# RWKV-6 recurrence and SwiGLU: k's product moves from VectorE to GpSimd, state scaling in one instruction, and a new order

## The chip, the cores and the metric

The kernel runs on one core of one Trainium2 chip. The metric is device time in microseconds: the median of the runs of one kernel. Inside a core five engines run their own instruction streams: PE (TensorE, matrix multiplications), DVE (VectorE), ACT (ScalarE), POOL (GpSimd) and SP (SyncE, which here only issues DMAs). PE writes to PSUM, eight banks of accumulator memory that DVE and ACT read.

## The reference

There are B = 4 batches, H = 8 heads, S = 768 time steps and D = 48 channels per head. For each batch and head a state of 48 x 48 numbers is carried through time, and its output is normalised and passed through a gated feed-forward layer:

```python
cur = np.einsum('bhd,bhe->bhde', u[None] * kt, vt)
y[:, :, t] = np.einsum('bhd,bhde->bhe', rt, state + cur)
state = wt[:, :, :, None] * state + np.einsum('bhd,bhe->bhde', kt, vt)
...
xn = x / np.sqrt(np.mean(x * x, axis=-1, keepdims=True) + 1e-06) * rms_g
g = xn @ w_gate
out = (g / (1.0 + np.exp(-g)) * (xn @ w_val)) @ w_out
```

Here x is y with the heads side by side: 3072 tokens by 384 channels. The hidden width is 1536.

## The kernel before

**Tiling.** Time is cut into six superblocks of 128 steps. A step of work is named `function.n.j`: superblock n (0 to 5), and batch j (0 to 3), or for the feed-forward layer one of 12 slices f of 128 hidden units. One tile holds 128 time steps on the partitions and 8 x 48 = 384 channels.

**The recurrence in matrix form.** The logarithm of w (`ln`) is summed over time by a matmul with a triangular mask (`cs_mm`, lines 350 to 376). This gives the exponent for r in a PSUM bank `ps_a` (line 369), and in four extra columns of the same bank the totals over the whole superblock (four small matmuls, line 372). The exponent for k lies in a bank `ps_b`: superblock 2 gets it by a second matmul with another mask (line 375), superblocks 3 to 5 (`ONE_SUM`) by adding ln w to r's sum on DVE (`cs_add`, line 380). Superblocks 0 and 1 (`WIN`) have their own matmuls. `exp_r` and `exp_k` (ACT, through line 200) take the exponentials: in place in PSUM, but for superblock 1 into SBUF tiles `er` and `ek`. `r_mul` (line 403) and `k_mul` (line 408), both on DVE, multiply r and k by them into the bf16 buffer `rk`. `w_tot` (line 400) copies the four totals into a small tile `wcol`.

**From there.** `rk` is transposed (`rk_tr`: for superblocks 0 and 1 by PE in `rk_pe` and a copy on ACT, later by a DMA on SP's queue, line 436), and `q_mm` (lines 449, 451) forms the products k.r of all pairs of time steps, for even and odd heads. `q_mask_e` (DVE, line 456) masks the even ones; `q_copy_o` (ACT) copies the odd ones out of PSUM and `q_mask_o` (POOL, line 467) masks them. `st_mm` (line 477) forms the sum of k v for the state. `st_new` adds the old state (line 483) and multiplies by the totals, in two DVE instructions of 48 partitions each (line 485): two heads lie together in one matmul, and only the two diagonal blocks are wanted. `y_mm` forms y. POOL computes the u term: `bonus_mul` (r k, then times u: lines 414 and 415), and after DVE's row sum `bonus_sum` (line 419) `bonus_v` (line 424). `x_add` adds both; `x_sq` (ACT), `x_rstd` (POOL, lines 515 and 516; ACT in superblock 0) and `xn_mul` (ACT) normalise. `xn_pe` and `xn_out`, or `xn_tr` and `xn_gain` with a DMA, transpose the result. POOL also casts v to bf16 (`cast_v`, from superblock 2).

**The feed-forward layer.** `gate_mm` and `val_mm` (line 557, three matmuls of 512 columns each) fill banks `ps_a` and `ps_b`; `silu` (ACT) and `h_mul` (DVE, line 575) make the hidden units; `o_mm` (line 620, twelve matmuls for each batch) projects them back, `o_out` copies and `out_dma` stores.

**What sets the order.** The string `ORDER` (lines 25 to 128) lists all 1091 steps. They are issued in just this order, so each engine and each DMA queue works through its own steps of the list, strictly in sequence, and waits where an input is late. The feed-forward layer of superblock n-1 is interleaved with the recurrence of superblock n. The list also has 36 `warm` steps: matmuls on zeros (line 333) which nobody reads. SP's queue carries the loads of r, k, v and w, the DMA transposes and the stores; POOL's queue carries the loads of the weights (`load_gv`, `load_wo`), which stand in POOL's sequence.

**PSUM.** Three pools of banks are handed out in rotation: `psA` (2 banks), `psB` (2) and `psQ` (4), lines 167 to 169.

Of the kernel before, what the change touches and what calls it, by code (L numbers as in the profile page):

```python
# [37 lines left out]
cast_v.0.2 cast_v.0.3 bonus_sum.0.2 bonus_sum.0.3 warm.27.0 x_add.0.0 warm.29.0 x_sq.0.0 load_r.2.3 r_mul.1.0 q_mm.0.2
q_mask_e.0.2 y_mm.0.1 cs_mm.1.1 x_rstd.0.0 exp_k.1.1 xn_mul.0.0 warm.35.0 x_add.0.1 q_mask_o.0.2 warm.34.0 q_mm.0.3
q_mask_e.0.3 x_sq.0.1 exp_r.1.1 x_rstd.0.1 load_k.2.3 y_mm.0.2 bonus_v.0.2 x_add.0.2 x_sq.0.2 xn_mul.0.1 x_rstd.0.2  # L40
xn_mul.0.2 q_mask_o.0.3 cs_mm.1.2 st_mm.0.3 st_mm.0.2 st_new.0.2 xn_pe.0.0 bonus_v.0.3 y_mm.0.3 x_add.0.3 load_gv.1.0
load_gv.1.1 bonus_mul.1.0 xn_out.0.0 xn_pe.0.1 xn_out.0.1 x_sq.0.3 x_rstd.0.3 xn_mul.0.3 xn_pe.0.2 xn_out.0.2 cs_mm.1.3
exp_r.1.3 exp_r.1.2 exp_k.1.3 xn_pe.0.3 st_new.0.3 k_mul.1.0 rk_pe.1.0 rk_tr.1.0 st_mm.0.1 xn_out.0.3 gate_mm.0.0
gate_mm.0.1 exp_k.1.2 q_mm.1.0 val_mm.0.1 k_mul.1.3 r_mul.1.3 silu.0.0 st_new.0.1 val_mm.0.0 rk_pe.1.3 q_mask_e.1.0
h_mul.0.0 k_mul.1.1 q_copy_o.1.0 silu.0.1 h_mul.0.1 gate_mm.0.2 silu.0.2 gate_mm.0.6 silu.0.6 val_mm.0.2 h_mul.0.2
bonus_sum.1.0 gate_mm.0.3 gate_mm.0.5 val_mm.0.3 silu.0.3 h_mul.0.3 cast_v.1.0 st_mm.1.0 gate_mm.0.9 st_new.1.0
silu.0.5 gate_mm.0.4 silu.0.9 r_mul.1.1 val_mm.0.5 h_mul.0.5 bonus_mul.1.3 gate_mm.0.7 rk_tr.1.3 cast_v.1.1 silu.0.4
val_mm.0.4 h_mul.0.4 st_mm.1.1 rk_pe.1.1 st_new.1.1 val_mm.0.9 val_mm.0.6 h_mul.0.6 r_mul.1.2 bonus_v.1.0 q_mask_o.1.0
y_mm.1.0 bonus_mul.1.1 k_mul.1.2 rk_tr.1.1 gate_mm.0.8 silu.0.8 silu.0.7 val_mm.0.7 h_mul.0.7 rk_pe.1.2 rk_tr.1.2
q_mm.1.1 q_copy_o.1.1 gate_mm.0.11 silu.0.11 load_wo.0.0 load_wo.2.0 q_mask_e.1.1 x_add.1.0 bonus_mul.1.2 load_wo.1.0  # L50
val_mm.0.8 h_mul.0.8 h_mul.0.9 q_mm.1.3 q_copy_o.1.3 q_mask_o.1.3 bonus_sum.1.3 q_mm.1.2 q_mask_e.1.2 q_copy_o.1.2
bonus_sum.1.1 gate_mm.0.10 val_mm.0.11 silu.0.10 val_mm.0.10 h_mul.0.10 bonus_sum.1.2 h_mul.0.11 q_mask_o.1.1 y_mm.1.1
x_sq.1.0 q_mask_o.1.2 cast_v.1.2 y_mm.1.2 bonus_v.1.1 x_add.1.1 o_mm.0.0 q_mask_e.1.3 ln.2.0 cs_mm.2.0 ln.2.1 cs_mm.2.1
bonus_v.1.2 x_add.1.2 o_out.0.0 out_dma.0.0 x_rstd.1.0 x_sq.1.1 cast_v.1.3 y_mm.1.3 st_mm.1.3 st_new.1.3 o_mm.0.1
bonus_v.1.3 x_rstd.1.1 x_add.1.3 exp_r.2.0 xn_mul.1.0 xn_pe.1.0 exp_k.2.1 k_mul.2.1 xn_mul.1.1 exp_r.2.1 w_tot.2.1
x_sq.1.2 x_rstd.1.2 r_mul.2.0 xn_out.1.0 w_tot.2.0 st_mm.1.2 st_new.1.2 o_mm.0.2 ln.2.2 cs_mm.2.2 x_sq.1.3 xn_mul.1.2
xn_pe.1.2 exp_k.2.0 k_mul.2.0 rk_tr.2.0 o_out.0.1 xn_pe.1.1 xn_out.1.1 xn_out.1.2 o_mm.0.3 exp_k.2.2 k_mul.2.2
load_v.2.0 r_mul.2.1 rk_tr.2.1 ln.2.3 x_rstd.1.3 exp_r.2.2 w_tot.2.2 xn_mul.1.3 xn_pe.1.3 xn_out.1.3 cs_mm.2.3
exp_r.2.3 r_mul.2.2 r_mul.2.3 w_tot.2.3 exp_k.2.3 k_mul.2.3 load_w.3.0 cast_v.2.1 st_mm.2.1 load_w.3.3 val_mm.1.1
gate_mm.1.1 silu.1.1 h_mul.1.1 o_out.0.2 load_v.2.2 rk_tr.2.3 load_v.4.3 rk_tr.2.2 load_v.2.3 load_k.3.1 load_r.3.1  # L60
o_out.0.3 out_dma.0.3 st_new.2.1 gate_mm.1.0 silu.1.0 val_mm.1.0 h_mul.1.0 bonus_mul.2.1 bonus_sum.2.1 gate_mm.1.5
silu.1.5 gate_mm.1.7 silu.1.7 val_mm.1.5 h_mul.1.5 bonus_mul.2.2 bonus_mul.2.0 bonus_v.2.1 gate_mm.1.3 silu.1.3
q_mm.2.0 q_mask_e.2.0 bonus_sum.2.2 q_mm.2.1 q_mask_e.2.1 gate_mm.1.2 silu.1.2 val_mm.1.2 h_mul.1.2 gate_mm.1.4
cast_v.2.0 st_mm.2.0 st_new.2.0 val_mm.1.3 h_mul.1.3 val_mm.1.4 gate_mm.1.6 bonus_mul.2.3 cast_v.2.2 st_mm.2.2
q_copy_o.2.1 bonus_sum.2.0 silu.1.4 h_mul.1.4 silu.1.6 q_copy_o.2.0 bonus_v.2.2 q_mask_o.2.0 q_mask_o.2.1 bonus_sum.2.3
cast_v.2.3 gate_mm.1.8 st_new.2.2 val_mm.1.7 gate_mm.1.9 h_mul.1.7 val_mm.1.9 y_mm.2.1 x_add.2.1 bonus_v.2.0 silu.1.9
h_mul.1.9 gate_mm.1.10 silu.1.10 y_mm.2.0 x_add.2.0 bonus_mul.3.1 val_mm.1.6 h_mul.1.6 q_mm.2.2 q_copy_o.2.2
q_mask_o.2.2 x_sq.2.0 q_mask_e.2.2 x_rstd.2.0 q_mm.2.3 q_mask_e.2.3 val_mm.1.8 val_mm.1.11 silu.1.8 h_mul.1.8
bonus_sum.3.1 bonus_v.2.3 q_copy_o.2.3 q_mask_o.2.3 load_r.3.0 load_k.3.0 bonus_mul.3.0 gate_mm.1.11 silu.1.11
h_mul.1.11 st_mm.2.3 y_mm.2.2 ln.3.0 val_mm.1.10 h_mul.1.10 o_mm.1.0 x_add.2.2 st_new.2.3 o_out.1.0 xn_mul.2.0 y_mm.2.3  # L70
x_add.2.3 cs_mm.3.0 xn_pe.2.0 cs_add.3.0 load_w.3.1 load_k.3.2 ln.3.1 cs_mm.3.1 cs_add.3.1 xn_out.2.0 out_dma.0.1
load_w.3.2 ln.3.2 x_sq.2.1 x_rstd.2.1 x_sq.2.2 load_k.3.3 out_dma.0.2 load_r.4.1 load_r.3.3 load_v.3.0 out_dma.1.0
load_v.3.2 load_r.3.2 exp_r.3.0 w_tot.3.0 bonus_sum.3.0 r_mul.3.0 ln.3.3 exp_k.3.1 exp_k.3.0 k_mul.3.0 rk_tr.3.0
# [58 lines left out]
def kernel(  # L132
# [42 lines left out]

    def sel(s):
        return {(int(x[0]), int(x[1])) for x in s.split()}

    CAST_ACT = sel("00 01 02 03 10 11 12 13")
    EXPR_SB = sel("10 11 12 13")  # L180
    EXPK_SB = sel("10 11 12 13")
    WIN = (0, 1)
    Q_PAIR = ((4, 2),)
    OLD_DVE = (1, 2, 3, 4)
    ONE_SUM = (3, 4, 5)
    O_IN_A = ()
    XOUT_ACT = sel("")
# [484 lines left out]
```

## Time and profile before

| quantity | value |
|---|---|
| median of 3 runs | 207.44 us (207.34 to 208.61) |
| the profiled execution | 208.67 us, of which the span from first to last instruction is 206.9 us; 1.8 us lie around it |
| mean granted TensorE clock | 0.992 |
| busy | PE 195.5, DVE 159.3, ACT 138.1, POOL 108.9 us |
| k_mul on DVE, 20 from PSUM and 4 from SBUF | 546 and 609 ns each |
| st_new's two multiplies, 40 in all | 354 ns each |
| r k on POOL (line 414), 24 | 999 ns each |
| HBM | 25.96 MB read, 4.72 MB written |

The profile is of one execution. Busy times of PE overlap, since matmuls are pipelined: a matmul's record is longer than the distance to the next one. A line of a group gives line, engine, operation, tiles, shapes and count, then busy us in all, mean ns of one, and the idle time of the engine just before. A line of windows gives the length of a stretch and each engine's busy us in it, with the number of instructions, then the granted clock, the share of the DMA engines and GB/s. A line of the timeline gives start us, length us, engine, line, operation, tiles and count.

The first matmul of line 557 starts at 31.63 us. The first matmul of each superblock's out projection (line 620) starts at 53.78, 84.63, 115.90, 144.73, 172.59 and 195.93 us. The stretches between these marks are called stages here: stage 1 from 53.78 (`o_mm.0.0`), stage 2 from 84.63 (`o_mm.1.0`), stage 3 from 115.90, stage 4 from 144.73, stage 5 from 172.59.

### The profile page before, as it was taken

Reading aid. Unit: us, or ns where it says so; the run is one execution under the profiler, and the core shown is the slowest. Engines: PE = TensorE matmul, PEld = TensorE weight load, DVE = VectorE, ACT = ScalarE, POOL = GpSimd, SP = SyncE. Lnnn points to the kernel's source line nnn. Section 1 sums busy time; section 2 is a strip of 40 time slices with the busy share of each in tenths; the row PEclk is TensorE's granted clock in tenths of the full one; section 3 lists DMA queues with packets and bytes.
Section 4 is the critical chain, followed back from the end, with each engine's and each line's share of the span. In section 5 each row is a group of like instructions: output and inputs, shape, how many; then the busy total and the mean of one; then the engine's idle time right before and its main releaser. Section 6 shows DMA issues by size and latency. Waiting matters only on the chain.

```text
span 206.9 us, 4493 instructions
## 1 busy us (share of the span) xinstructions
PE 195.5 (94%) x1608; PEld 114.8 (55%) x1608; DVE 159.3 (77%) x324; ACT 138.1 (67%) x278; POOL 108.9 (53%) x170
## 2 busy tenths in 40 slices
PE   1999969989999999999999999999999999999994
PEld 1566545555665555665546665556555556555562
DVE  5169895789998899999879999998986676236521
ACT  2587998557997645889557968576976666064400
POOL 6098980390959379739776859738330464000000
PEclk9999997999999999999999999999999999999999
DMA  6999999999996999969989989982128401140013
GB/s 139 287 229 188 186 213 203 189 197 207 202 210 134 204 212 222 204 142 197 204 156 262 196 193 244 199 160 47 22 76 212 105 5 38 38 155 0 0 55 137
DMA packets 121566, 32.41 MB, mean 157 GB/s; under 512 B 116420, under 2 KB 120392, under 8 KB 121544
## 3 DMA queue, kind: packets, MB, share of 16 engines
q1 hardware_dynamic: 119504, 28.58, 64.4%
q0 software_dynamic: 2032, 3.54, 9.4%
q8 instruction: 12, 0.20, 0.4%
q14 instruction: 10, 0.08, 0.1%
q10 hardware_dynamic: 8, 0.00, 0.0%
HBM read 25.96 MB, written 4.72 MB: 148 GB/s over the span
## 4 chain that ended last, share of the span: by engine, by line
PE 50%; DVE 14%; DMA 9%; ACT 9%; POOL 6%; SPq 6%; issue 6%; DVEq 0%; POOLq 0%; ACTq 0%
PE ps_q L620 13%; PE ps_a L557 13%; PE ps_b L557 12%; DMA rt<-in_r_dram 7%; DVE ht L575 3%; SPq L213 3%; DMA vt<-in_v_dram 2%; DVE st L485 2%; PE ps_q L449 2%; ACT xn L520 2%; SPq L226 2%; PE ps_q L431 2%; POOL qts L467 1%; POOL ruk L415 1%; PE ps_q L333 1%
## 5 line engine op out<-in xcount | busy, mean ns | idle before, releaser
L200 ACT ACTIVATE sg<-ps_a 128x512 bf16<-128x512 f32 x72 | 42.1, 598 | 38.3 <-PE ps_a L557 27.9
L575 DVE TENSOR_TENSOR ht<-ps_b,sg 128x512 bf16<-128x512 f32 x72 | 48.6, 686 | 20.6 <-ACT sg L200 10.9
L557 PE MATMUL ps_b<-xnt,wv_sb 128*128 128x512 bf16 x216 | 56.5, 380 | 1.0 <-DVE ht L575 0.7
L557 PE MATMUL ps_a<-xnt,wg_sb 128*128 128x512 bf16 x216 | 56.0, 385 | 0.1
L620 PE MATMUL ps_q<-wo_sb,ht 128*128 128x384 bf16 (+1 forms) x300 | 49.4, 320 | 0.2 <-ACT ob L629 0.2
L620 PEld LDWEIGHTS <-ht 128*128 128x128 bf16 x300 | 28.2, 98 | 17.1 <-issue 0.2
L557 PEld LDWEIGHTS <-wg_sb 128*128 128x128 bf16 x216 | 23.4, 115 | 20.6 <-issue 1.6
L557 PEld LDWEIGHTS <-wv_sb 128*128 128x128 bf16 x216 | 22.9, 114 | 20.2 <-issue 2.6
L414 POOL TENSOR_TENSOR ruk<-rt,kt 128x384 f32<-128x384 f32 x24 | 24.0, 999 | 13.7 <-DVE rk L403 6.3
L424 POOL TENSOR_TENSOR ydiag<-vt,diag 128x384 f32<-128x384 f32 x24 | 20.0, 839 | 12.9 <-DVE diag L419 12.8
L415 POOL TENSOR_TENSOR ruk<-ruk,u_bc 128x384 f32<-128x384 f32 x24 | 24.0, 999 | 1.9
L467 POOL TENSOR_SCALAR_AFFINE_SELECT qts<-qts 128x512 bf16<-128x512 bf16 x20 | 12.4, 634 | 19.0 <-ACT qts L460 19.0
L456 DVE TENSOR_TENSOR qts<-ps_q,mask_lt 128x512 bf16<-128x512 f32 x24 | 16.2, 681 | 1.5 <-PE ps_q L451 1.4
L520 ACT ACTIVATE xn<-xb,rstd 128x384 bf16<-128x384 f32 x24 | 14.4, 611 | 3.8 <-POOL rstd L516 3.6
L502 DVE TENSOR_TENSOR xb<-ps_q,ydiag 128x384 f32<-128x384 f32 x24 | 13.2, 549 | 1.5 <-PE ps_q L497 1.4
L198 ACT ACT_TABLE_LOAD x10 | 12.8, 1283 | 1.8 <-PEq L656 1.6
L419 DVE TENSOR_REDUCE diag<-ruk 128x8 f32<-128x384 f32 x24 | 13.0, 544 | 1.1 <-POOL ruk L415 1.0
L403 DVE TENSOR_TENSOR rk<-rt,ps_a 128x384 bf16<-128x384 f32 x20 | 10.8, 545 | 3.6 <-ACT ps_a L200 3.5
L507 ACT ACTIVATE junk<-xb 128x384 bf16<-128x384 f32 x24 | 12.4, 517 | 1.6 <-DVE xb L502 1.3
L200 ACT ACTIVATE lw<-wt 128x384 bf16<-128x384 f32 (+1 forms) x20 | 11.0, 577 | 3.6 <-DMA wt<-in_w_dram 3.5
L515 POOL TENSOR_SCALAR rstd<-rstd 128x1 f32<-128x1 f32 x20 | 3.8, 190 | 16.5 <-ACT junk L507 15.6
L460 ACT CAST qts<-ps_q 128x512 bf16<-128x512 f32 x20 | 11.3, 585 | 1.0 <-PE ps_q L451 0.8
(83 smaller groups left out, 281.5 us busy)
## 6 DMA issues: line engine op xcount, KB each, us to landing
rt<-in_r_dram SPq DMA_DIRECT2D x24, 192.0 KB, 4.0
kt<-in_k_dram SPq DMA_DIRECT2D x24, 192.0 KB, 3.7
vt<-in_v_dram SPq DMA_DIRECT2D x24, 192.0 KB, 3.6
out_dram<-ob SPq DMA_DIRECT2D x23, 192.0 KB, 2.1
wt<-in_w_dram SPq DMA_DIRECT2D x16, 192.0 KB, 3.6
wt<-in_w_dram SPq DMA_DIRECT2D x4, 384.0 KB, 4.6
wo_sb<-in_moe_w_out_dram POOLq DMA_DIRECT2D x3, 384.0 KB, 7.1
wg_sb<-in_moe_w_gate_dram POOLq DMA_DIRECT2D x1, 768.0 KB, 10.0
```

The costliest lines, as they stand in the source:

```text
L200: return nc.scalar.activation(**kw).ins
L414: nc.gpsimd.tensor_tensor(out=ruk[n, j], in0=inp["r", n, j], in1=inp["k", n, j], op=ALU.mult)
L415: nc.gpsimd.tensor_tensor(out=ruk[n, j], in0=ruk[n, j], in1=u_bc, op=ALU.mult)
L419: nc.vector.tensor_reduce(out=diag[n, j].rearrange("p h o -> p (h o)"), in_=ruk[n, j], axis=mybir.AxisListType.X, op=ALU.add)
L424: nc.gpsimd.tensor_tensor(out=ydiag[n, j], in0=inp["v", n, j], in1=diag[n, j].to_broadcast([128, H, D]), op=ALU.mult)
L456: nc.vector.tensor_tensor(out=qts[n, j][:, 0], in0=bank["q", n, j][0], in1=bc_mid(mask_lt, NP), op=ALU.mult)
L467: nc.gpsimd.affine_select(out=qts[n, j][:, 1], in_=qts[n, j][:, 1], compare_op=ALU.is_gt, fill=0.0, base=0, pattern=[[0, NP], [1, 128]], c ...
L502: nc.vector.tensor_tensor(out=xb[n, j], in0=bank.pop(("y", n, j)), in1=ydiag[n, j].rearrange("p h d -> p (h d)"), op=ALU.add)
L520: nc.scalar.activation(out=xn, in_=xb[n, j], func=AF.Copy, scale=rstd[n, j][:, 1:2])
L557: nc.tensor.matmul(ps, lhsT=units(ws, c, f), rhs=xnt[n][:, c, :], start=(c == 0), stop=(c == KC - 1))
L575: nc.vector.tensor_tensor(out=ht[n][:, f, :], in0=bank.pop(("v", n, f)), in1=bank.pop(("sg", n, f)), op=ALU.mult)
L620: nc.tensor.matmul(ps[:, cols], lhsT=ht[n][:, f, b * L:(b + 1) * L], rhs=wo_sb[:, f, cols], start=(f == 0), stop=(f == FC - 1))
```

## The change

Six things change. First, `k_mul` of superblocks 2 to 5 (16 instructions) runs on POOL, and so their `exp_k` writes its result to SBUF (tile `ek`, four buffers) and not in place in PSUM. Second, `w_tot` writes eight columns, the totals times 1 or 0 by half of the partitions, and `st_new` multiplies all 128 partitions in one instruction; the unwanted blocks are multiplied by 0. Superblock 1 gets a `w_tot` too (four more). Third, superblock 2 joins `ONE_SUM`: its mask matmul (line 375) goes, four `cs_add` come. Fourth, superblock 5 has no totals any more (16 small matmuls of line 372 go). Fifth, PSUM banks are no longer handed out in rotation: from the list of steps the program knows each bank's last use, and gives out the bank whose last use is earliest. Sixth, `ORDER` is a new list of the same steps, with the four `cs_add` and four `w_tot` added.

```diff
-    psA = ctx.enter_context(tc.tile_pool(name="psA", bufs=2, space=bass.MemoryType.PSUM))
-    psB = ctx.enter_context(tc.tile_pool(name="psB", bufs=2, space=bass.MemoryType.PSUM))
-    psQ = ctx.enter_context(tc.tile_pool(name="psQ", bufs=4, space=bass.MemoryType.PSUM))
+    psP = ctx.enter_context(tc.tile_pool(name="psP", bufs=1, space=bass.MemoryType.PSUM))
...
-    EXPK_SB = sel("10 11 12 13")
+    K_POOL = sel("20 21 22 23 30 31 32 33 40 41 42 43 50 51 52 53")
+    EXPK_SB = sel("10 11 12 13") | K_POOL
...
-    ONE_SUM = (3, 4, 5)
+    ONE_SUM = (2, 3, 4, 5)
...
+    rings = {"a": [[-2, 0], [-2, 1]], "b": [[-2, 0], [-2, 1]], "q": [[-2, 0], [-2, 1], [-2, 2], [-2, 3]]}
+    def psum(ring, key, shape, dtype=FP32):
+        slots = rings[ring]
+        k = min((x for x in range(len(slots)) if slots[x][0] < at[0]), key=lambda x: slots[x])
+        taken[0] += 1
+        slots[k] = [last_use.get(key, -1), taken[0]]
+        return psP.tile(shape, dtype, name="ps_" + ring + "uvxz"[k])
...
+        last = n == NSB - 1
         nc.tensor.matmul(a[:, NP:NP + DM].rearrange("p (h d) -> p h d", h=H), lhsT=mask_lt, rhs=rhs,
-                         start=True, stop=False)
-        for q in range(NP):
+                         start=True, stop=last)
+        for q in range(0 if last else NP):
...
     def w_tot(n, j):
-        wcol[n, j] = small.tile([128, NP], FP32, name="wcol", bufs=12)
-        nc.vector.tensor_copy(out=wcol[n, j], in_=bank["cs_r", n, j][:, 0:NP])
+        wcol[n, j] = small.tile([128, NP, 2], FP32, name="wcol", bufs=12)
+        nc.vector.tensor_tensor(out=wcol[n, j], in0=bank["cs_r", n, j][:, 0:NP].unsqueeze(2).to_broadcast([128, NP, 2]),
+                                in1=bc_mid(half_of, NP), op=ALU.mult)
...
     def k_mul(n, j):
-        nc.vector.tensor_tensor(out=rk[:, n % 2, j, 1, :, 0:D], in0=inp["k", n, j],
+        eng = nc.gpsimd if (n, j) in K_POOL else nc.vector
+        eng.tensor_tensor(out=rk[:, n % 2, j, 1, :, 0:D], in0=inp["k", n, j],
...
-        for p0, c0 in ((0, 0), (PD, D)):
-            nc.vector.tensor_tensor(
-                out=new[p0:p0 + D, :, c0:c0 + D], in0=ps[p0:p0 + D, :, c0:c0 + D],
-                in1=wc[p0:p0 + D, 0:NP].to_broadcast([D, NP, D]), op=ALU.mult)
+        nc.vector.tensor_tensor(out=new.rearrange("p q (c d) -> p (q c) d", c=2),
+                                in0=ps.rearrange("p q (c d) -> p (q c) d", c=2),
+                                in1=wc.rearrange("p q c -> p (q c)").unsqueeze(2).to_broadcast([128, 2 * NP, D]),
+                                op=ALU.mult)
```

Of the new `ORDER`, five parts matter below. SP's list begins `load_k.0.1 load_w.0.0 load_w.0.1 load_k.0.0 load_v.0.0 load_w.0.3 load_r.0.0` (before: `load_r.0.0 load_k.0.1 load_w.0.0 load_w.0.1 load_v.0.0 load_w.0.3 load_k.0.0`). PE's list begins with 13 `warm` steps ahead of `cs_mm.0.0` (before: 5), and has 4 between `rk_pe.0.2` and `y_mm.0.0` (before: 8). ACT's list has `exp_k.1.1` and `exp_r.1.1` ahead of `x_sq.0.0` (before: behind it), and `cast_v.0.0` behind `exp_r.0.0` (before: ahead). POOL's list up to the second weight group was

```
bonus_v.0.1 bonus_v.0.2 bonus_v.0.3 load_gv.1.0 load_gv.1.1 bonus_mul.1.0 bonus_mul.1.3
```

(with `load_gv.0.1` and `load_gv.0.0` among the `bonus_v`), and now is

```
bonus_v.0.0 load_gv.0.0 bonus_v.0.2 bonus_v.0.3 load_gv.0.1 bonus_mul.1.0 load_gv.1.0 bonus_mul.1.1 load_gv.1.1
```

POOL's list of stage 2, from `o_mm.1.0` to `o_mm.2.0`, now begins

```
bonus_v.2.2 bonus_v.2.3 q_mask_o.2.3 x_rstd.2.1 bonus_mul.3.0 x_rstd.2.2 x_rstd.2.3 k_mul.3.0 cast_v.3.1 bonus_v.3.0
cast_v.3.2 k_mul.3.1 cast_v.3.0 bonus_v.3.1 k_mul.3.2 bonus_mul.3.3 bonus_mul.3.2 k_mul.3.3 q_mask_o.3.0 ...
```

## The prediction

> **What bounds the kernel now.** I read the page's busy times first, then the windows by stage, then the groups by form, then the timeline of PE and the waits of POOL.
>
> ```profile
> PE 195.5 (94%) x1608; PEld 114.8 (55%) x1608; DVE 159.3 (77%) x324; ACT 138.1 (67%) x278; POOL 108.9 (53%) x170
> ```
> ```profile
> 0.00:31.60 31.60, 25.05 (x268) 15.85 (x269) 22.52 (x50) 22.58 (x49) 21.88 (x35) 0.98 1.03 207
> 57.12:84.80 27.68, 27.39 (x226) 15.84 (x224) 25.56 (x55) 19.04 (x39) 20.22 (x32) 1.00 0.94 200
> 84.80:115.80 31.00, 30.44 (x272) 17.96 (x271) 29.12 (x63) 24.08 (x50) 22.18 (x33) 1.00 0.93 191
> 115.80:145.40 29.60, 29.43 (x246) 17.33 (x244) 27.70 (x59) 21.34 (x44) 21.26 (x33) 1.00 0.82 168
> 145.40:172.75 27.35, 27.14 (x219) 15.42 (x217) 21.59 (x42) 20.10 (x44) 9.88 (x19) 1.00 0.32 83
> ```
> Columns: stretch, its length, busy us of PE, PEld, DVE, ACT, POOL. PE is the bound from 31.6 us on. DVE is close behind it in stage 2 (29.12 of 31.00 us, 94%), where POOL has 72%. Before 31.6 us PE waits for the others.
>
> Busy PE is not PE at its peak, so I count the work of stage 2 by distances between starts: 24 feed-forward products at 0.65 us, 4 projections at 1.95, 5 `y_mm` at 0.37, 6 `cs_mm` at 0.26, 5 `xn_pe` at 0.17, 4 `q_mm` at 0.32, 4 `st_mm` at 0.17: 29.6 us of the 31.27 between 84.63 and 115.90. So PE stalls 1.65 us there; counted alike, 1.3 us in stage 1 (30.85 us), 1.0 in stage 3 (28.83), 0.7 in stage 4 (27.86), about nothing in stage 5. Only these 4.65 us, the start, and matmuls that go can be won.
>
> ```profile
> L408 DVE TENSOR_TENSOR rk<-kt,ps_b 128x384 bf16<-128x384 f32 x20 | 10.8, 546 | 1.4 <-ACT ps_b L200 1.3
> L485 DVE TENSOR_TENSOR st<-ps_q,wcol 48x192 bf16<-48x192 f32 x32 | 11.3, 354 | 0.6
> L380 DVE TENSOR_TENSOR ps_b<-ps_a,lw 128x384 f32<-128x384 f32 x12 | 6.4, 557 | 0.1
> L542 DVE TENSOR_TENSOR xnt<-ps_q,gT 128x384 bf16<-128x384 bf16 x16 | 8.5, 550 | 0.1
> L414 POOL TENSOR_TENSOR ruk<-rt,kt 128x384 f32<-128x384 f32 x24 | 24.0, 999 | 13.7 <-DVE rk L403 6.3 <-DMA kt<-in_k_dram 3.7 <-DMA rt<-in_r_dram 3.6
> ```
> ```profile
> 5.94 1.78 PE L333 MATMUL ps_q<-junk 128*128 128x384 bf16 x5
> 7.51 0.85 PE L355 MATMUL ps_a<-lw,mw 128*128 128x384 bf16 x2
> ...
> 56.00 0.32 PE L375 MATMUL ps_b<-lw,mask_nle 128*128 128x384 bf16 x1
> 56.16 0.32 PE L369 MATMUL ps_a<-lw,mask_lt 128*128 128x384 bf16 x1
> ```
> ```profile
> 147.21 0.24 PE L372 MATMUL ps_a<-ones_col,lw 128*128 128x1 bf16 x4
> 147.31 0.32 PE L369 MATMUL ps_a<-lw,mask_lt 128*128 128x384 bf16 x1
> ```
> ```profile
> POOL rstd L515 <- ACT junk L507: 5.0, 3, 2.8
> POOL qts L467 <- ACT qts L460: 1.9, 1, 1.9
> POOL ruk L414 <- DMA rt<-in_r_dram: 0.9, 1, 0.9
> ```
> The last fence is POOL's waits within stage 2 alone.
>
> **The change, part by part.**
>
> *Matmuls that go.* The mask matmul of line 375 takes 0.16 us of PE from start to start, four totals of line 372 take 0.10. Four of each: 0.64 + 0.40 = **-1.05 us**, at 56 to 65 and 147 to 152 us, where PE is the path. Bounds: -1.05, and 0 if PE would only wait there.
>
> *DVE is relieved.* Sixteen products at 0.546 are 8.7 us less; twenty `st_new` save 2 x 0.354 - 0.55 (from line 542, same shape and types) = 0.16 each, 3.2 in all. Four `cs_add` at 0.557 and four `w_tot` at 0.15 come: +2.8. So DVE falls by 9.1 to 150.2 us. Superblock 2, in stage 1, gains only 0.6, since four `cs_add` take the place of four products; superblocks 3 and 4 gain 2.8 each. In stage 2 DVE falls from 29.1 to about 26.3 of 31 us. Of PE's 1.65 us of stalls there I take three quarters, **-1.25 us**: DVE is the fullest engine beside PE, but some of PE's waits there name ACT. Bounds: -1.65 and 0. In stages 1, 3 and 4 I take nothing (bound -3.0, all their stalls), since the same superblocks load POOL.
>
> *POOL is loaded.* A product of two f32 tiles of 384 takes 0.999 us there (line 414): sixteen are 16.0 us, 108.9 becomes 124.9. The product now ends 0.45 us later after `exp_k` than on DVE, and `exp_k` to SBUF takes 493 ns where in place it took 472. For superblock 2 `cs_add` adds 0.56 us more. Behind the product stand the DMA transposes on SP (3.2 us to landing in the trace), behind these SP's next loads; then `q_mm`, and POOL's own `bonus_v`, `q_mask_o` and `x_rstd`, for which PE's `y_mm` and ACT's `xn_mul` wait. I add up the new POOL list of stage 2 from its start: `k_mul.3.0` ends at 7.6 us and `cast_v.3.0` at 10.9, where PE's list has 11.3 us of work ahead of `st_mm.3.0`; `k_mul.3.3` ends at 17.7 and `q_mask_o.3.0` at 18.4, and PE's list has 18.4 ahead of `y_mm.3.0`. So it just fits, with no reserve: I take **0**. Bounds: 0, and +5.6, worked out under the rivals.
>
> [...]
>
> *The start, to 31.63 us.* PE's five fillers ahead of `cs_mm.0.0` took 0.32 us each (5.94 to 7.51). With 13 it starts at about 5.94 + 13 x 0.32 = 10.1 us, or a little less if the clock rises as it did at about 9.6 us; so `exp_r.0.0`, which ran at 9.43, moves to about 10.6: +1.1 us. Against it four fillers fewer stand ahead of `y_mm.0.0` (0.16 to 0.38 us each, 0.6 to 1.5), and two exponentials (0.9 us of ACT) leave the normalising chain of 22.6 to 30.1 us, which ended last; `cast_v.1.0` enters it (0.5). On SP, r of superblock 0 goes from first to seventh and k from seventh to fourth; POOL needs both, and the later one stays seventh, so nothing. Bounds: -1.5 (fillers and exponentials cashed) and +1.1. Middle: **-0.2**.
>
> *The weights.* The second value group was issued at 25.51 us on POOL and landed 13.6 later, at 39.06; its first use began at 41.45. Now two `bonus_mul` (four instructions of 1.0) stand ahead: issue at about 29.7, landing at 43.3 if it takes as long, at 39 if the DMA engines' total was what held it. The first use in the new list has the same 12 products ahead and two small steps more: about 42.2. Bounds: 0 and +1.1; I take **+0.4**, nearer to 0 since in 31.6 to 57.1 us the DMA engines were busy throughout (share 1.06).
>
> *PSUM banks.* PE's waits for a bank show only as 0.7 us on `h_mul` and 0.2 on a copy; earliest-last-use can win these 0.9 and lose as much. I take 0. With `exp_k` in SBUF, `ps_b` comes free one step sooner; hidden behind PE.
>
> Sum: -1.05 - 1.25 + 0 - 0.2 + 0.4 = **-2.1 us**. Against the profiled execution this is 208.67 - 2.1 = 206.6, span 204.8; that execution lies 1.2 us above the median, so for the median 207.44 - 2.1 = **205.3 us**.
>
> **The rivals.**
>
> *DVE's relief pays in every stage.* For it: DVE is 92 to 94% busy in stages 1 to 3. Then stalls of 3.0 us more, less 1 which stay, and 1.3 more from the start: 205.3 - 2.0 - 1.3 = 202.0.
>
> *PE's work alone.* For it: PE idles little in stages 1 to 4 (1.2 us by the windows), and its stalls could simply move. Then -1.05 and the weights' 0.4: 206.8.
>
> *POOL becomes the bound in stage 2 (slower).* The new list holds 6 `bonus_v`, 5 `q_mask_o`, 6 `x_rstd`, 5 `bonus_mul`, 4 `k_mul`, 5 `cast_v` between `o_mm.1.0` and `o_mm.2.0`: 5.0 + 3.2 + 4.4 + 10.0 + 4.0 + 2.5 = 29.1 us (23.1 before). POOL takes its list in sequence and waited 7.8 us in this stage. If the 5.0 us on the squares stay, it needs 34.1, 2.8 more than the stage; if all stay, 36.9, 5.6 more. With -1.05 and +0.4 this is 209.6, at worst 212.4. It decides once more than 2.2 us of waits remain (31.3 - 29.1). Against it: what POOL has left can spill into stage 3, whose new list is lighter, 20 us.
>
> **How the numbers follow.** A measurement here can tell about 1% (2.1 us, so 205.4 and 209.5) from no change. The forecast gets 0.46, its own range 203.3 to 206.9, of which 0.29 lies under 205.4 and 0.17 above. All stages: 0.17, faster. PE alone: 0.15, within 1%. POOL: 0.22, of which 0.02 within 1%. So faster 0.46, same 0.34, slower 0.20. The range reaches from 201.5, just under the first rival, to 210.0, past the middle of the last: about 2 in 10 stay outside.
>
> **What would show it.** Right: DVE near 150 and POOL near 125 us busy; line 408 on POOL at about 1.0 us; stage 2 at about 29.5 to 30 us with DVE at 26; the first matmul of line 557 at 30 to 32.5 us. Wrong: waits of PE for POOL's `qts` or for `rk`, or POOL over 95% busy in stage 2; `cs_mm.0.0` at 10 us with the first product after 33; a wait of a product for `wv_sb` near 42 us.

## The result and the profile after

The changed kernel takes 204.65 us (median of 4 runs, 204.20 to 204.97) against 207.39 us in the same comparison: 0.9836 of before, with an interval of 0.9805 to 0.9867. A second comparison gave 0.982 (0.9788 to 0.9852). The forecast was 205.3 us. The profiled execution after took 204.97 us, its span is 203.3 us; the span of before was 206.9 us. About 1.2 us of that difference is most likely no work of the change: the profiled execution of before had a granted clock of 0.83 between 30 and 40 us and lay 1.2 us above its median. Two kernels below (experiment 5's first, experiment 6's second) have profiled executions with a lower clock, 3 to 4 us above their undisturbed ones; of these only waits and stages at full clock are read.

The first fence is the line of busy times of the page after. The second holds the windows of the trace after, cut at the same places as the stages of before: the stretch, its length, busy us of PE, PEld, DVE, ACT and POOL, the clock, the DMA share, GB/s. The five lines are the way from the first product to `o_mm.0.0`, then stages 1 to 4.

```profile
PE 189.9 (93%) x1569; PEld 113.1 (56%) x1588; DVE 154.2 (76%) x299; ACT 137.7 (68%) x278; POOL 125.4 (62%) x186
```
```profile
31.57:52.87 21.30, 19.80 (x154) 11.09 (x158) 19.78 (x34) 15.95 (x30) 10.02 (x14) 1.00 1.10 205
52.87:82.56 29.69, 29.53 (x267) 17.90 (x269) 26.48 (x54) 22.66 (x47) 24.88 (x36) 1.00 0.96 181
82.56:112.27 29.71, 29.38 (x277) 18.10 (x277) 26.42 (x54) 23.68 (x48) 26.32 (x38) 1.00 0.96 198
112.27:140.01 27.74, 27.53 (x232) 16.44 (x234) 23.36 (x47) 20.66 (x45) 22.41 (x34) 1.00 1.01 219
140.01:168.95 28.94, 27.22 (x206) 15.52 (x208) 23.94 (x42) 21.34 (x45) 18.37 (x28) 1.00 0.31 80
```

| stretch | before | after | difference |
|---|---|---|---|
| start, to the first product | 31.63 | 31.57 | -0.06 |
| first product to `o_mm.0.0` | 22.15 | 21.30 | -0.85 (the clock of before was 0.96 here: about 0.9 us) |
| stage 1 | 30.85 | 29.69 | -1.16 |
| stage 2 | 31.27 | 29.71 | -1.56 |
| stage 3 | 28.83 | 27.74 | -1.09 |
| stage 4 | 27.86 | 28.94 | **+1.08** |
| stage 5 and the end | 34.28 | 34.30 | 0 |

Three stages gained 3.8 us, and one gave 1.1 back. In stage 2 DVE has 26.42 us and POOL 26.32, as forecast. But DVE in all has 154.2 us, not 150.2. Most of the 4 us is in three groups that read nothing but SBUF. Two of them before (mean ns behind the busy time; the third, k's product of superblock 1, took 609 ns), and then the groups of the trace after:

```profile
L403 DVE TENSOR_TENSOR rk<-rt,er 128x384 bf16<-128x384 f32 x4 | 3.2, 796 | 0.0
L546 DVE TENSOR_SCALAR xnt<-xnt,gT 128x512 bf16<-128x512 bf16 x6 | 1.7, 346 | 3.8 <-DMA xnt<-xn 3.8
```
```profile
L438 DVE TENSOR_TENSOR rk<-rt,er 128x384 bf16<-128x384 f32 x4 | 3.8, 945 | 0.0
L444 DVE TENSOR_TENSOR rk<-kt,ek 128x384 bf16<-128x384 f32 x4 | 3.2, 808 | 0.0
L582 DVE TENSOR_SCALAR xnt<-xnt,gT 128x512 bf16<-128x512 bf16 x6 | 3.6, 655 | 3.7 <-DMA xnt<-xn 3.5 <-issue 0.2
L444 POOL TENSOR_TENSOR rk<-kt,ek 128x384 bf16<-128x384 f32 x16 | 15.9, 1001 | 1.1 <-ACT ek L230 1.1
```

The product on POOL takes 1001 ns, as POOL's row of before said. The gain `xn_gain` (line 582; 346 ns before) now takes 655 in the mean and up to 1048, though no line of it changed: 1.9 us in all. The r and k products of superblock 1 (lines 438 and 444) take 1.4 us more than before, and one r product among the four takes 2134 ns. The wider `w_tot`, 3.7 us where the forecast's terms make 3.0, is the rest. The gain's delay and the r product's reach PE, whose waits after begin, behind the one at the very start, with:

```profile
PE ps_bu L593 <- DVE xnt L582: 1.5, 2, 1.3
PE ps_qx L467 <- DVE rk L438: 1.2, 1, 1.2
```

The timeline after at the first of these places (start us, length us, engine):

```profile
146.91 1.96 POOL L444 TENSOR_TENSOR rk<-kt,ek 128x384 bf16<-128x384 f32 x2 [0.22 <-ACT ek L230]
...
147.97 2.72 DVE L582 TENSOR_SCALAR xnt<-xnt,gT 128x512 bf16<-128x512 bf16 x3 [0.20 <-issue]
...
148.82 2.55 POOL L460 TENSOR_TENSOR ydiag<-vt,diag 128x384 f32<-128x384 f32 x3
...
150.61 0.54 DVE L438 TENSOR_TENSOR rk<-rt,ps_au 128x384 bf16<-128x384 f32 x1
```

Three gains that took 0.87 us in the trace of before (from 153.31 us on) take 2.72 while POOL works on k's products and `bonus_v` without a pause. The r product right behind them, with one input in PSUM, takes its usual 0.54 beside the same POOL work. PE waits 1.5 us for these gains, more than stage 4's loss. At the second place the slow r product starts when POOL has begun a `bonus_v`, and ends 0.4 us after POOL's next instruction has ended, so it waits for two:

```profile
44.12 0.91 POOL L460 TENSOR_TENSOR ydiag<-vt,diag 128x384 f32<-128x384 f32 x1
44.28 2.13 DVE L438 TENSOR_TENSOR rk<-rt,er 128x384 bf16<-128x384 f32 x1
45.01 0.98 POOL L450 TENSOR_TENSOR ruk<-rt,kt 128x384 f32<-128x384 f32 x1
```

### The profile page after: what moved, and what is told of

It reads as the page before. It is cut to its first block, busy times and chain, and to the rows that moved or that the text cites. A ratio compares the mean times of both kernels' runs of the same rounds, so it can differ in the third digit from the quotient of the medians.

```text
span 203.3 us, 4409 instructions
## 1 busy us (share of the span) xinstructions
PE 189.9 (93%) x1569; PEld 113.1 (56%) x1588; DVE 154.2 (76%) x299; ACT 137.7 (68%) x278; POOL 125.4 (62%) x186
## 4 chain that ended last, share of the span: by engine, by line
PE 84%; ACT 6%; DVE 3%; issue 2%; POOL 1%; DMA 1%; POOLq 0%; DVEq 0%
PE ps_bv L593 12%; PE ps_au L593 12%; PE ps_av L593 10%; PE ps_bu L593 10%; PE ps_qu L625 7%; PE ps_qx L625 5%; PE ps_qv L625 4%; PE ps_qz L625 4%; PE ps_qx L367 1%; DVE rk L438 1%; ACT xn L556 1%; ACT junk L543 1%; DMA xnt<-xn 1%; PE ps_qv L485 1%; PE ps_qu L467 1%
## 5 line engine op out<-in xcount | busy, mean ns | idle before, releaser
L230 ACT ACTIVATE sg<-ps_au 128x512 bf16<-128x512 f32 x38 | 22.8, 599 | 17.4 <-PE ps_au L593 13.9
L611 DVE TENSOR_TENSOR ht<-ps_bv,sg 128x512 bf16<-128x512 f32 x38 | 26.1, 688 | 9.3 <-PE ps_bv L593 5.1
L230 ACT ACTIVATE sg<-ps_av 128x512 bf16<-128x512 f32 x34 | 20.4, 600 | 16.1 <-PE ps_av L593 9.7
L593 PE MATMUL ps_bv<-xnt,wv_sb 128*128 128x512 bf16 x110 | 30.7, 380 | 0.3
L593 PE MATMUL ps_au<-xnt,wg_sb 128*128 128x512 bf16 x110 | 30.5, 380 | 0.4
L611 DVE TENSOR_TENSOR ht<-ps_bu,sg 128x512 bf16<-128x512 f32 x34 | 23.3, 686 | 9.2 <-ACT sg L230 6.0
L593 PE MATMUL ps_bu<-xnt,wv_sb 128*128 128x512 bf16 x94 | 27.1, 380 | 2.0 <-DVE xnt L582 1.5
L593 PE MATMUL ps_av<-xnt,wg_sb 128*128 128x512 bf16 x99 | 27.3, 380 | 0.1
L625 PE MATMUL ps_qu<-wo_sb,ht 128*128 128x384 bf16 x96 | 16.9, 326 | 0.0
L444 POOL TENSOR_TENSOR rk<-kt,ek 128x384 bf16<-128x384 f32 x16 | 15.9, 1001 | 1.1 <-ACT ek L230 1.1
```

The source lines that it names most:

```text
L230: return nc.scalar.activation(**kw).ins
L444: eng.tensor_tensor(out=rk[:, n % 2, j, 1, :, 0:D], in0=inp["k", n, j], in1=bank["cs_k", n, j][:, 0:DM].rearrange("p (h d) -> p h d", h=H) ...
L593: nc.tensor.matmul(ps, lhsT=units(ws, c, f), rhs=xnt[n][:, c, :], start=(c == 0), stop=(c == KC - 1))
L611: nc.vector.tensor_tensor(out=ht[n][:, f, :], in0=bank.pop(("v", n, f)), in1=bank.pop(("sg", n, f)), op=ALU.mult)
L625: nc.tensor.matmul(ps[:, cols], lhsT=ht[n][:, f, b * L:(b + 1) * L], rhs=wo_sb[:, f, cols], start=(f == 0), stop=(f == FC - 1))
```

## The experiments

The theory after the comparison: DVE's relief pays in stages 1 to 3, the matmuls that went pay their time, and stage 4 loses because DVE and POOL keep each other off SBUF, as the times above suggest (2.72 against 0.87 us); experiment 1 tests that. The rivals: the order alone or the matmuls alone make the gain, and the long gains come of late transposes.

**1. DVE and POOL side by side.** A kernel that computes nothing of the reference. Its four operations, each of which stands in loops of 12 or 24 (the notes behind `#` are not in the code):

```diff
+    V.tensor_scalar(out=gain_alone, in0=bf, scalar1=sc, scalar2=None, op0=ALU.mult)   # 128x512 bf16
+    V.tensor_tensor(out=rsb_alone, in0=f1, in1=f2, op=ALU.mult)                       # two SBUF inputs
+    V.tensor_tensor(out=rps_alone, in0=f1, in1=ps, op=ALU.mult)                       # one PSUM input
+    G.tensor_tensor(out=pool_alone, in0=f3, in1=f4, op=ALU.mult)
```

> This kernel leaves out the whole of the computation. It times by themselves, twelve at a time, three VectorE operations of the kernel (the gain, 128x512 bf16 by a column, SBUF to SBUF; the r product with both inputs in SBUF; the r product with one input in PSUM) and GpSimd's product from SBUF (128x384 f32 to bf16); then each of the three, 24 times, beside twelve of GpSimd's products. Theory (the two engines keep each other off SBUF where VectorE reads nothing but SBUF): the gain alone about 345 ns, beside GpSimd 600 ns or more; the product from SBUF alone about 546, beside GpSimd 750 or more; the product from PSUM about 550 alone and beside GpSimd; GpSimd alone 1000 ns, longer beside the first two. Rival (the long gains and products of the changed kernel come of something else, such as transposes landing late or DMA traffic): all three the same alone and beside GpSimd, within 5%.

The compiler mixed the groups, so that "alone" and "beside" must be read from the timeline and not from the tile names. Three places of it: POOL busy throughout; POOL idle; and the product from PSUM beside POOL, with a gain behind it.

```profile
10.99 1.30 POOL L76 TENSOR_TENSOR pool_gain<-f,f 128x384 bf16<-128x384 f32 x1
11.36 1.08 DVE L61 TENSOR_SCALAR gain_alone<-bf,sc 128x512 bf16<-128x512 bf16 x1
12.25 1.04 POOL L68 TENSOR_TENSOR pool_alone<-f,f 128x384 bf16<-128x384 f32 x1
12.36 1.34 DVE L63 TENSOR_TENSOR rsb_alone<-f,f 128x384 bf16<-128x384 f32 x1
...
24.15 0.34 DVE L61 TENSOR_SCALAR gain_alone<-bf,sc 128x512 bf16<-128x512 bf16 x1
24.41 0.55 DVE L63 TENSOR_TENSOR rsb_alone<-f,f 128x384 bf16<-128x384 f32 x1
...
33.41 1.04 POOL L90 TENSOR_TENSOR pool_rps<-f,f 128x384 bf16<-128x384 f32 x1
33.51 0.54 DVE L65 TENSOR_TENSOR rps_alone<-f,ps 128x384 bf16<-128x384 f32 x1
33.98 0.61 DVE L74 TENSOR_SCALAR gain_both<-bf,sc 128x512 bf16<-128x512 bf16 x1
```

The gain takes 0.34 us alone and 1.08 beside POOL; the product of two SBUF tensors 0.55 and 1.34; the product with one input in PSUM 0.54 either way. A DVE instruction of the first two kinds starts 0.93 us before the end of the POOL instruction beside it and ends 0.15 and 0.41 us after that end (12.44 against 12.29, 13.70 against 13.29): most of its time is a wait for POOL's. In this stretch the two take turns, one instruction each, and POOL's product, 0.99 us while DVE is idle, takes 1.04 and 1.30. What a gain costs depends on how much of POOL's instruction is left: the last row's starts 0.57 us into one and takes 0.61, again ending 0.14 after it, and one at 29.60 us, which starts 0.15 us into one, takes 0.99. The theory holds as far as these times go, and the rival falls; 1.08 and 1.34 us are above the 0.60 and 0.75 expected at the least. The rows show the wait and its size; what makes it they do not show.

**2. POOL quiet during the gains.** The five POOL steps go behind the last gain in the list, and the first product of k among them waits for it (`behind` makes one instruction wait for another):

```diff
+        if (n, j) == (5, 1):
+            behind(i, gain[-1])
```

> The changed kernel with GpSimd kept quiet while VectorE does the three gains of superblock 4: cast of v 5.0, k's products 5.1 and 5.0 and the v products 5.0 and 5.2 come behind the last gain, and the first of k's products waits for it. Theory (the two engines share the way to SBUF, and this made the 1.5 us of stage 4): gains at 340 to 360 ns, TensorE's wait for the gain before the first value matmul of superblock 4 under 0.4 us in place of 1.5, and 203.1 to 203.9 us. Rival 1 (the gains are late for another reason): 204.4 to 205.0 us, gains long still. Rival 2 (k's products, about 1.5 us later, now hold up the transposes of superblock 5 and the products of stage 4): gains short, a wait for the transposed rk instead, 204.2 us or more.

203.91 us, 0.9788 of before (0.9769 to 0.9807). The timeline of this kernel:

```profile
147.68 0.88 DVE L585 TENSOR_SCALAR xnt<-xnt,gT 128x512 bf16<-128x512 bf16 x3
...
148.69 1.97 POOL L445 TENSOR_TENSOR rk<-kt,ek 128x384 bf16<-128x384 f32 x2 [2.05 <-ACT ek L230]
```

The three gains take 0.88 us, stage 4 is 27.78 us long in place of 28.94, and PE's wait for the gain is gone. The products of k, 1.8 us later than in the kernel after, cost PE 0.4 us in one wait for a transposed `rk`. Rival 1 falls; rival 2 is real but small. By the ratios this is 0.7 to 1.0 us under the changed kernel, within the intervals of both; it is the trace that shows the gain in stage 4.

**3. POOL quiet at the r product too.**

```diff
+        if (n, j) == (1, 1):          # bonus_v.1.1
+            behind(i, rmul[1, 2])
```

> The kernel with the gains first (203.91 us), and also GpSimd's v product 1.1 held until VectorE's r product 1.2 is done. Theory (that product reads two SBUF tensors and took 2.1 us beside GpSimd, TensorE waiting 1.2 to 1.3 us for it): the product at 0.55 us, the wait under 0.3 us, 202.5 to 203.1 us. Rival 1 (the product was slowed by DMA traffic, or the wait passes to the next step on VectorE): 203.7 to 204.2 us. Rival 2 (GpSimd's later v products and masks now hold up superblock 1): 204.3 us or more.

202.82 us, 0.9724 (0.968 to 0.9767). To set it beside the changed kernel on one chip, both were run once more:

> The changed kernel as it is, as the base for the three runs beside it on this chip: 0.980 to 0.987 of the kernel before, as in its first comparison.

> The kernel with GpSimd kept quiet at both places (the gains of superblock 4, the r product 1.2), again, now beside the changed kernel on one chip. Theory (both waits were the shared way to SBUF): 1.5 to 2.5 us under the changed kernel. Rival (the differences of the earlier runs were the chip's): within 0.7 us of it.

The changed kernel took 204.33 us (0.982, 0.9788 to 0.9852), this one **202.09 us (0.971, 0.9681 to 0.9739)**: 2.2 us less, the fastest of all kernels here. In its windows the stretch ahead of `o_mm.0.0` and stage 4 are the ones that differ from the kernel after:

```profile
32.02:51.54 19.52, 19.36 (x153) 10.99 (x157) 17.51 (x34) 16.00 (x29) 9.58 (x14) 1.00 1.08 198
...
138.67:166.36 27.69, 27.23 (x207) 15.63 (x208) 22.08 (x42) 21.32 (x45) 18.17 (x28) 1.00 0.32 82
```
```profile
44.09 0.55 DVE L440 TENSOR_TENSOR rk<-rt,er 128x384 bf16<-128x384 f32 x1
```

19.52 against 21.30 us, with 0.55 us for the r product in place of 2.13, and 0.55 for k's product just ahead of it in place of 1.17; 27.69 against 28.94. DVE's busy time in stage 4 falls from 23.94 to 22.08 us without one instruction less. The start of this execution was 0.45 us longer than that of the kernel after, so the span shows less than the sum of the two.

**4. The edits in the order of before.** `cs_add.2.j` is put behind `cs_mm.2.j`, `w_tot.1.j` behind `exp_r.1.j`, and the rest of the list is that of before:

```diff
-cs_mm.2.0
+cs_mm.2.0 cs_add.2.0
...
-exp_r.1.0
+exp_r.1.0 w_tot.1.0
```

> All edits of the change in the order of before, with the new steps (k sums of superblock 2 by add, the total's step of superblock 1) put right behind the steps that feed them. Theory (matmuls that go, 1.05 us, and VectorE's relief work in any order): 205.0 to 206.0 us. Rival (the gain beyond the matmuls is the new order's): 206.2 to 207.5 us, stages 1 to 3 as long as before less 0.16 us for each mask matmul.

**224.5 us**, 1.0785 of before (1.0754 to 1.0817). Neither theory had this. PE's waits in this kernel name POOL (`PE ps_qu L514 <- POOL vb L375: 3.3`) and ACT's xn (7.4 us in several waits). POOL's timeline at one of them:

```profile
63.48 1.00 POOL L445 TENSOR_TENSOR rk<-kt,ek 128x384 bf16<-128x384 f32 x1 [1.07 <-ACT ek L231]
64.55 0.19 POOL L552 TENSOR_SCALAR rstd<-rstd 128x1 f32<-128x1 f32 x1
64.83 0.55 POOL L553 TENSOR_TENSOR rstd<-rstd,mhalf 128x1 f32<-128x1 f32 x1
...
68.47 0.99 POOL L445 TENSOR_TENSOR rk<-kt,ek 128x384 bf16<-128x384 f32 x1 [3.10 <-ACT ek L231]
69.41 0.50 POOL L375 CAST vb<-vt 128x384 bf16<-128x384 f32 x1
```

A product of k stands at the head of POOL's queue and waits for its exp, 1.07 us and later 3.10; behind it stand the two small rstd instructions, for which ACT's xn and then PE's transposes wait, and the cast, for which PE's `st_mm` waits. POOL is not full (26.8 of 37.9 us in this stage): it is blocked. In the list of before, `k_mul.2.1` stands ahead of `x_rstd.1.2`, `k_mul.3.0` ahead of `x_rstd.2.2`, `k_mul.4.0` ahead of `x_rstd.3.3`; in the new list all rstd steps of a superblock stand ahead of all products of the next.

**5. The product back on DVE, in both orders.** One line, in the changed kernel and in the kernel of experiment 4. `exp_k` still writes to SBUF, so the product on DVE now reads two SBUF tensors, where in the kernel before it read one from PSUM. (The new order allows nothing else: with `exp_k` in place in PSUM, both `ps_b` banks are still in use when `val_mm.2.7` needs one.)

```diff
-        eng = nc.gpsimd if (n, j) in K_POOL else nc.vector
+        eng = nc.vector
```

> The changed kernel with its order as it is, and only the engine of k's product of superblocks 2 to 5 put back to VectorE (the exp still lands in SBUF). VectorE gets 16 products of 0.55 us or more back, 4 a superblock. Theory (VectorE's relief is what shortens stages 1 to 3, the shared way to SBUF gives part of it back): stage 2 at 30.5 to 31.5 us against 29.7, stages 1 and 3 longer by 0.3 to 1.2 us each, the gains of superblock 4 at 350 ns and stage 4 shorter by about 1 us; 205.3 to 207.0 us. Rival (the order and the matmuls that went are the whole gain): 203.2 to 204.9 us, that is the same, or the 1 us of stage 4 better.

> All edits in the order of before as in the run that took 224.5 us, but k's product on VectorE. Theory (in the order of before a product on GpSimd that waits for its exp holds up the small rstd steps, casts and masks that stand behind it in GpSimd's queue, and through them ScalarE's xn and TensorE's transposes): without it the time falls to 205.5 to 208.5 us. Rival (the PSUM bank rule, or the k sums of superblock 2 by add, do not suit the order of before): 215 us or more.

In the new order 218.55 us, 1.0477 (1.0428 to 1.0526); in the order of before 212.6 us, 1.0153 (1.0098 to 1.0209). So in the order of before the product on POOL costs 12 to 13 us (224.5 to 212.6, or the ratios), which speaks for the queue and against the bank rule and the adds as the main cause. About 2.8 us of it is the clock of 0.50 after one long stop of PE (an estimate, last section). But the 205.5 to 208.5 us of the theory were missed: with the other edits alone that order is still 1.5% over before. And in the new order having the product on POOL is worth not 1 or 2 us but 13 to 14. PE's waits in stages 1 and 4 of it:

```profile
PE ps_bu L593 <- DVE xnt L582: 3.1, 1, 3.1
```
```profile
PE ps_au L404 <- DVE rk L438: 2.1, 1, 2.1
PE ps_bv L593 <- DVE xnt L578: 2.1, 1, 2.1
```

The products stand ahead of the steps that PE needs in DVE's queue now: `k_mul.5.1` and `k_mul.5.0` stand between the first and the second gain. DVE is busy 2.75, 2.30, 2.51 and 2.54 us longer than after in stages 1 to 4, with four instructions more in each: 0.58 to 0.69 us for one product from SBUF (an estimate from the windows of both kernels), against 0.546 from PSUM before. So part of the loss may be the wait beside POOL of experiment 1; how much was not measured. Stage 2, at full clock, is 30.90 us long with DVE at 28.7: 1.2 us more than after, the size that the forecast had for stage 2. Stage 3, also at full clock, is 2.53 us longer. The rest came in stages 1 and 4, where PE's waits are those above and the clock is 0.95 and 0.90. The rival that the order makes the gain alone falls, and so does any reading by which engine and order add up: each is bad without the other.

**6. Places in POOL's queue.** From experiment 4, seven products (2.0, 2.1, 2.2, 3.0, 3.1, 4.0, 4.1) and, where needed, the transposes behind them, go behind the last `x_rstd` of the superblock before:

```diff
-x_rstd.1.0 x_rstd.1.1 k_mul.2.1 x_rstd.1.2 k_mul.2.0 k_mul.2.2 x_rstd.1.3 k_mul.2.3
+x_rstd.1.0 x_rstd.1.1 x_rstd.1.2 x_rstd.1.3 k_mul.2.1 k_mul.2.0 k_mul.2.2 k_mul.2.3
```

(steps of other engines between them left out)

> All edits in the order of before (224.5 us), with seven of k's products of superblocks 2 to 4, and the transposes behind them where needed, moved back to where all rstd steps of the superblock before have been issued; in the order of the change all sixteen stand so. Theory (a product that waits for its exp at the head of GpSimd's queue holds the rstd steps behind it, and TensorE then waits for xn): 207 to 214 us, TensorE's waits for xn under 2 us in place of 7.4. Rival 1 (the casts, masks and transposes matter as much): 214 to 220 us. Rival 2 (the PSUM bank rule or the adds do not suit that order): over 220 us.

219.06 us, 1.0525 (1.049 to 1.0561): 5.4 us less, with PE's waits for xn in stages 1 to 3 down from 6.0 us to 0.3, and the 3.3 us for the cast still there. That is what rival 1 expected. Then one step more:

```diff
-k_mul.2.3 cast_v.2.1
+cast_v.2.1 k_mul.2.3
```

(POOL's steps alone)

> The kernel in the order of before with k's products behind the rstd steps (219.06 us), and one step moved besides: the cast of v 2.1 ahead of k's product 2.3, which stood at the head of GpSimd's queue for 2.7 us waiting for its exp, while TensorE waited 3.3 us for the cast behind it. Theory (it is the place in GpSimd's queue): TensorE's wait of 3.3 us for the cast is gone, and the lower granted clock behind it with it (0.95 over stage 1); 2.5 to 5 us less, 214 to 216.5 us. Rival (the next step on the same path, the product 2.3 itself or its transposes, comes just as late): 218 us or more.

1.038 of before (1.0326 to 1.0434), that is 215.4 us on 207.54: about 3 us by the ratios for one step's place in a list, inside what the theory expected. The wait for the cast falls from 3.3 to 0.9 us, and stage 1 is 33.18 us long, at full clock, in place of 35.50 at a clock of 0.95, which alone is about 1.7 us (an estimate from its windows, 0.82 from 69 to 73 us and 0.75 from 73 to 77). A wait of 2.5 us for a transposed `rk` and others stay; 11 us over the new order are not traced further.

**7. Two multiplies for the state.** With them `w_tot` copies the four totals again, and superblock 1 has none.

```diff
+        for p0, c0 in ((0, 0), (PD, D)):
+            nc.vector.tensor_tensor(out=new[p0:p0 + D, :, c0:c0 + D], in0=ps[p0:p0 + D, :, c0:c0 + D],
+                in1=wc[p0:p0 + D, 0:NP].to_broadcast([D, NP, D]), op=ALU.mult)
```

> The changed kernel with the new state made by two multiplies of half the partitions again (2 x 0.354 us against 0.557), the totals copied and not widened. VectorE gets about 0.15 us for each of 20 states, 0.6 us a superblock, and saves four 0.27 us steps in superblock 1. Theory (where VectorE is 26.4 of 29.7 us busy some of its time shows at the end, but not all): 0.2 to 1.0 us more than the changed kernel. Rival (TensorE alone sets the time): within 0.2 us of it.

207.06 us (0.9963, 0.9939 to 0.9988), 2.7 us more than the changed kernel beside it. The windows of stages 1 and 2 of this kernel:

```profile
52.76:83.21 30.45, 29.89 (x266) 17.89 (x268) 27.85 (x60) 22.73 (x48) 25.08 (x36) 1.00 1.01 187
83.21:113.52 30.31, 29.84 (x276) 18.23 (x276) 27.32 (x58) 23.69 (x48) 26.32 (x38) 1.00 0.98 194
```

They are 0.76 and 0.60 us longer than after, stage 3 0.21, stage 4 nothing. DVE is busy 1.37 and 0.90 us longer in these two stages, so 0.55 to 0.67 of DVE's time reaches the end there. The spans differ by 1.6 us; the other 1.1 us of the medians lies in which executions were profiled, this one 0.7 us under its median and the changed kernel's 0.4 over. Theory right in kind, too small in size; the rival that PE alone sets the time falls.

**8. The matmuls back.** `ONE_SUM = (3, 4, 5)`, `last = False`, `exp_r` over the totals' columns too, and no `cs_add.2.j`.

> The changed kernel with the removed matmuls back: the mask matmul of superblock 2 (in place of its four adds on VectorE) and the totals of superblock 5. TensorE gets 4 x 0.16 and 4 x 0.10 us back; VectorE loses four adds of 0.56 us in stage 1. Theory (TensorE never waits long, so its work is the time): 0.8 to 1.2 us more, 205.4 to 205.9 us. Rival (VectorE sets stage 1 as well, so the four adds that go give 0.5 us or more back): 204.4 to 205.2 us.

206.58 us, 0.9889 (0.9846 to 0.9931). By the ratios this is 1.1 to 1.4 us over the changed kernel, near the 0.8 to 1.2 expected and barely clear of the intervals (0.9 us either way), but the trace puts it elsewhere than the theory did. Stage 1 is 0.48 us longer than after (four mask matmuls of 0.16 are 0.64), although DVE has 1.4 us less to do there: no sign of the rival. The totals of superblock 5 cost stage 4 nothing: 28.92 us with them, 28.94 without. And stage 3, where no matmul came back, is 1.04 us longer; ACT waited 1.2 us there for a load of w that landed late, and PE 0.8 us behind it. Why it landed late is open.

## Why the prediction was right, and where it was not

The total was right by 0.65 us, its terms less so.

- *Matmuls that go, -1.05:* the four mask matmuls gave 0.48 of 0.64 us (experiment 8). The totals gave 0 of 0.40 in the kernel as it is, the bound that the step named for a PE that only waits: PE waits for the gain in that stage, 1.5 us without the totals and 1.3 with them.
- *DVE is relieved, -1.25 in stage 2 and nothing elsewhere:* the mechanism was right, the size was off. Stage 2 gave 1.56. **The failed part is "In stages 1, 3 and 4 I take nothing"**: stages 1 and 3 gave 1.16 and 1.09, of which the mask matmuls explain 0.5 in stage 1. In stages 1 and 2 the state's single multiply alone is worth 0.76 and 0.60 (experiment 7). The thought behind the zero, that the same superblocks load POOL, was wrong for stages 1 and 3: POOL had room (24.88 of 29.69 us and 22.41 of 27.74). Of stage 3's 1.09 the single multiply is 0.21; the rest is not taken apart.
- *POOL is loaded, 0:* right for the queue, and the list added up by hand ("it just fits") was the right test: `k_mul.3.0` ended 7.9 us into stage 2 (7.6 was said), `k_mul.3.3` 17.8 (17.7), `q_mask_o.3.0` 18.4 (18.4). POOL waited 1.8 us in stage 2 after, 7.8 before, and is 89% busy there. What it would have cost otherwise was a bound of 5.6 us by a full POOL; the order of before shows 12 to 13 us by a blocked one. The rival of a bound POOL looked at POOL's sum of work, and the price was in who stands behind whom.
- *What no step had:* that DVE's instructions which read nothing but SBUF wait for POOL's (the gain 0.34 us alone, 1.08 beside POOL, in experiment 1). DVE's and POOL's durations were taken as fixed. A sign was in the trace of before: its four r products from SBUF (line 403) took 546, 714 and 1212 ns (least, median, most), while those from PSUM all took about 546. The change put POOL's new products and `bonus_v` beside the gains: +1.1 us in stage 4. The r product's 2.1 us ahead of stage 1 is of the same kind, though POOL has no new product there and only the order changed; taking it away gave another 1.8 us in that stretch (experiment 3).
- *The start, -0.2:* -0.06. `cs_mm.0.0` started at 10.09 us, as worked out (10.1), `exp_r.0.0` at 11.17 (10.6 was said; the matmul started at 10.09 still took 0.53 us, where the forecast let matmuls be faster from about 9.6 on). The forecast put that down to a clock that rises at about 9.6 us; in the trace of before the granted clock is 1.00 on both sides of it (9.0 to 9.6 us, 9.6 to 10.5), and what changes is the distance between the starts of fillers, 0.32 us up to 9.65 and 0.16 from 11.03 on. After, it is 0.32 up to 10.09 and 0.16 from 12.41 on. What sets the moment is not shown.
- *The weights, +0.4:* 0. Issued at 30.45 us (29.7 was said), they landed 9.8 us later (13.6 before), ahead of their use near 42 and nearer to the 39 us that the step had for the case that the DMA engines' total held them than to its 43.3. Taken without the clock of before, the stretch neither gained nor lost; the 1.8 us that it could have gained went to the r product and k's before it.
- *PSUM banks, 0:* no wait of PE for a bank of note appears after; the 0.7 us on `h_mul` is gone, by the rule or by DVE's relief. The bank rule by itself wasn't tried, nor the new list with the engines of before.

So the sum came out near by luck: errors of both signs met. Stages 1 to 3 gave 1.9 us more than DVE's and the mask matmuls' terms had (3.8 against 1.25 + 0.64), and the weights' 0.4 was not lost; against it stand 1.5 us in stage 4 (0.40 to be gained, 1.08 lost) and 0.1 at the start. That is 0.7, about the 0.65 by which the kernel was faster than forecast. The rival "DVE's relief pays in every stage" (202.0) described stages 1 to 3; with POOL kept quiet at two places the kernel does take 202.1 us, but partly by a wait that this rival did not count.

## What to carry to other kernels

When work moves from VectorE to GpSimd, don't take either engine's durations as fixed: list the VectorE instructions that read nothing but SBUF (here the product of two tensors, 0.55 us alone and 1.34 beside GpSimd, and the bf16 scaling, 0.34 and 1.08) and see what GpSimd will run beside them; keeping GpSimd quiet at two places was worth 2.2 us here. Then go through the receiving engine's queue step by step: a waiting instruction at its head delays whatever small step stands behind it (here a cast of 0.50 us, for which TensorE waited 3.3), and the engine's busy share tells nothing of that (26.8 of 37.9 us). An order made for one assignment of engines is no fair test of another: test both together.

## What the hardware showed

- DVE's gain 0.34 us alone, 1.08 beside POOL; a product of two SBUF tensors 0.55 and 1.34; from PSUM 0.54 both times; POOL's product 1.0 alone and up to 1.3 (experiment 1). The gain's price followed from what was left of POOL's instruction when it started (0.99 us when it started 0.15 us into one, 0.61 when 0.57 us). Not expected was that the slower of the two sets the pace where they take turns (10.99 to 13.70 us in experiment 1): the gain of 0.34 us took 1.08, three times its length, and in the changed kernel one product, 2.13 us long, waited for two of POOL's instructions.
- After PE had stood still for 3.3 us (66.7 to 70.0 us in experiment 4), it worked at a granted clock of 0.50 until about 75.7 us; in windows of 4 us:

```profile
66.00:70.00 4.00, 0.62 (x9) 0.49 (x10) 2.11 (x5) 2.18 (x4) 1.53 (x3) 0.85 1.09 220
70.00:74.00 4.00, 4.00 (x13) 1.56 (x13) 0.33 (x1) 0.96 (x2) 3.84 (x5) 0.50 0.84 175
74.00:78.00 4.00, 4.00 (x16) 1.72 (x14) 3.19 (x7) 1.80 (x4) 2.91 (x4) 0.79 0.98 218
```

The clock is the number behind POOL's. By the 0.85 of the first window it fell at about 68.8 us, 2.2 us into the stop, and by the 0.79 of the third it came back at about 75.7 (estimates, if it was 0.50 or 1.00 throughout). At 0.50 three matmuls of 512 columns took 1.28 us from start to start (70.24 to 71.52 us); at 1.00, in stage 2 of before, they took 0.65 (95.74 to 96.39). So this wait cost about 2.8 us beyond its length (an estimate, half of the 5.7 us from 70.0 on). How long a stop it takes, and whether a stop is the cause, is not settled here. After one of 2.1 us in the same execution the clock did not fall: it is 1.00 from 91.47 to 187.01 us, and the 0.91 from 53.56 to 91.47 is no more than the 6.9 us above account for. Experiment 6's second kernel has one of 2.5 us and a clock of 0.95 from 88.88 to 123.21 us, as much as 3.4 us at 0.50 would make (an estimate). And in the trace of before the clock was 0.50 from 30.2 to 33.6 us, with no stop of PE over 0.6 us in the 10 us ahead: 3.4 us, half as long as the stretch in experiment 4.
